# The last stage's plain transfers go from SyncE's queue to GpSimd's, and the order planner gets new transfer costs

## The chip, the cores and the metric

The kernel runs on one core of a Trainium2 chip. The core has five engines that run side by side: TensorE (PE, with its weight loads shown as PEld), VectorE (DVE), ScalarE (ACT), GpSimd (POOL) and SyncE (SP). SyncE does nothing but issue transfers. Transfers between HBM and the on-chip memory (SBUF) are carried out by 16 DMA engines, which serve several queues; in the profile q1 is the queue that SyncE feeds, q10 ScalarE's, q0 GpSimd's, and q8 brings instructions. The metric is the device time of one execution in microseconds (us).

## The reference: what is computed

The forward pass and all gradients of a layer with two branches, for 2048 tokens (S) of 512 channels (D) in bf16:

```python
xn = _layernorm(x)                            # x = A_q
k_shift = sum over 4 lags of k shifted * shift_k
kv  = k_shift * v
y   = causal convolution of kv with ssm_k along the sequence (by FFT of length 4096) + kv * ssm_D
s   = xn * y
h   = sigmoid(xn @ w_gate) * (xn @ w_up)      # F = 1376
g   = silu(h @ w_down)
out = x + s * g
_grads = vjp(grad_out)   # of A_q, A_k, A_v, A_shift_k, A_ssm_k, A_ssm_D, w_gate, w_up, w_down
```

Outputs: out_0 is the result, out_1 to out_3 the gradients of q, k and v (2048 x 512 each), out_4 to out_6 those of the short filter, of ssm_k (512 x 2048) and of ssm_D, out_7 and out_8 those of w_gate and w_up (512 x 1376), out_9 that of w_down (1376 x 512).

## The kernel before, in words

Channels are worked in four groups of 128 (GW, index cg), tokens in eight pairs of 128-token tiles (index q). The FFT is done as matmuls with constant matrices; a group's spectrum is made in two halves, so there are eight spectral tiles n = 2 cg + u. There are three stages.

Stage A (forward) interleaves three streams (L1028): strG (layer norm, gate and up products, one q at a time), strK (spectra of ssm_k) and strV (shifted k, kv, its spectra, and the convolution). It stores to scratch in HBM what is needed again: h to hS_d, the sigmoids to sF_d, both spectra to KK_d (eight tiles of 1 MB), the shifted k to ksh_d.

Stage B (stepB, L1179) goes over the eight q: z_gen makes the gate and the gradient behind it, d_gen the gradients of the gate and up products (stored to dgS_d and duS_d), x_gen the gradient to x (out_1).

The last stage has three streams again. `dW` (L1217) makes the weight gradients out_9, out_7 and out_8 in nine jobs (s, c): s picks hS_d, dgS_d or duS_d, c one of three column chunks of 512, 512 and 352 (CH, L1205). Each job first needs a transposing load of its chunk from HBM (ld_L, L1208, 2 MB for a 512-wide chunk), which goes into one of two buffers, three once job 2 is through; a job frees its buffer and so lets the load three jobs (at first two jobs) later start. A job has four blocks (job 2 has three) of 16 accumulating matmuls; each block is copied out of PSUM into one of three small buffers (ot_r, L1387) and stored (L1243, L1245). `frontC` (L1274) makes the spectra Y of the gradient of the convolution's output. `backC` (L1288) takes for each n the tile KK(n) that ld_KK (L1253) loads into one of two buffers, multiplies both of its halves by Y on VectorE (L1302 to L1306, called M(n) here), and turns the products back with TensorE (inv3, inv1n, inv1). For each pair of groups `taps` (L1324) then makes the gradients of v (out_3), k (out_2) and the short filter; it needs v, k and the shifted k, loaded by ld_bwd (L1263) and ld_ksh (L1259). In the last stage SyncE issues all of these loads and stores; only the eight small copies inside SBUF at L1331 and L1332 are GpSimd's.

The order in which each engine's queue holds its instructions is not the program's. All operations are recorded (class Rec, L163), with a rank that run_streams (L559) gives by mixing the streams: a stream's tuple holds the work that it has, and the times at which it should begin and end as shares of the stage (the numbers at L1400 and L1415 to L1416). Then `order` (L348) plays all engines forward with the estimated costs of `cost` (L291) for compute and `dcost` (L328) for transfers, and takes on every engine the operation of the lowest rank that is ready. That order is emitted (L545) as a fixed program; each engine then does its instructions strictly in that order, and waits at each for what it needs. Line L553 issues all of TensorE's bursts and L555 everything else, so nearly every row of the profile has one of these two lines. A transfer costs the planner the time by which it holds its issuing queue and the time that it holds the DMA engines; `dcost` gives both from the size, the length of the contiguous runs, and the issuing engine:

```python
if "transpose" in meth:
    return (1.4 if str(src.space) != "DRAM" else nb / 215e3), nb / 256 * 18 / 16e3
...
pk = nb / run
d = pk * max(8 + 0.0375 * run, 18) / min(16, pk) / 1e3
```

Of the kernel before, what the change touches and what calls it, by code (L numbers as in the profile page):

```python
# [15 lines left out]
DRAM = bass.MemoryType.DRAM  # L16
# [11 lines left out]
GW = D // NG  # L28
# [134 lines left out]
class Rec:  # L163
# [164 lines left out]
    def dcost(self, alt):  # L328

        eng, meth, a, k = alt  # L330
        dst, src = a[0], a[1]
        nb = math.prod(dst.shape) * esize(dst.dtype)
        if "transpose" in meth:
            return (1.4 if str(src.space) != "DRAM" else nb / 215e3), nb / 256 * 18 / 16e3
        run = 4096 if eng == "sync" else 1 << 13
        for v in (dst, src):
            dims = [d for d in v.ap if d[1] > 1]
            r = 1
            for s, n in reversed(dims if str(v.space) == "DRAM" else [d for d in v.ap[1:] if d[1] > 1]):
                if s != r:  # L340
                    break
                r *= n
            run = min(run, r * esize(v.dtype))
        pk = nb / run
        d = pk * max(8 + 0.0375 * run, 18) / min(16, pk) / 1e3
        return (0.58 + max(0, pk - 256) * 3e-4 if eng == "gpsimd" else 0.55 if eng == "scalar" else 0.36 + max(0, pk - 128) * 6e-4), d

    def order(self):  # L348
# [210 lines left out]
def run_streams(streams, until=None):  # L559

    live = [list(st) + [0.0] * (5 - len(st)) for st in streams]
    while live:
        if until is not None and until():
            break
        for st in sorted(live, key=lambda s: s[2] + (s[3] - s[2]) * s[4] / s[1]):
            try:
                c = next(st[0])
            except StopIteration:
                live.remove(st)
                break  # L570
            if c:
                st[4] += c
                break
        else:
            raise RuntimeError("all streams blocked")
    return live
# [68 lines left out]
def kernel_impl(ctx, tc, A_q, A_k, A_v, A_shift_k, A_ssm_k, A_ssm_D, B_x, B_w_gate, B_w_up, B_w_down,  # L645
                grad_out, out_0, out_1, out_2, out_3, out_4, out_5, out_6, out_7, out_8, out_9):
    nc = tc.nc
    qC, kC, vC, goC = cview(A_q), cview(A_k), cview(A_v), cview(grad_out)
# [3 lines left out]
    ksh_d = dram.tile([NG, P, NJ, GW], bf16, name="ksh_d")  # L652
# [12 lines left out]
    def dma2(eng, dst, src, lo=None):  # L665
        if lo is None:
            for r in range(2):
                eng.dma_start(dst[64 * r:64 * r + 64], src[r])
# [201 lines left out]
    def ld_kh(eng, kh, c0, c1):  # L870
        nc.gpsimd.memset(kh[0:1, 0:3, :], 0.0)
        dma2(eng, kh[:, 3:, :], kC[:, :, :, c0:c1])
        eng.dma_start(kh[64:128, 0:3, :], kC[0, :, 13:16, c0:c1])
        eng.dma_start(kh[1:64, 0:3, :], kC[1, 0:63, 13:16, c0:c1])
# [342 lines left out]
    def dW():  # L1217
        for n, (s, c) in enumerate(jobs):
            f0, w = CH[c]
            while ("L", n) not in stC:  # L1220
                yield 0
            blk = stC.pop(("L", n))
            L = blk.ap
            nblk = -(-w // 128) if s == 0 else 4
            for b in range(nblk):
                acc = nc.ps("hi", [512], f32)
                kf = min(128, w - b * 128) if s == 0 else 128
                wo = D if s == 0 else w
                for j0 in range(0, NJ, 2):
                    calls = []  # L1230
                    for j in (j0, j0 + 1):
                        kw = dict(start=(j == 0), stop=(j == NJ - 1))
                        if s == 0:
                            calls.append(("matmul", (acc[0:kf, :], L[:, j, b * 128:b * 128 + kf], dzA[:, j, :]), kw))
                        else:
                            calls.append(("matmul", (acc[:, 0:w], xnA[:, j, b * 128:(b + 1) * 128], L[:, j, 0:w]), kw))
                    nc.burst("full", 2 * (wo / 2400 + 0.0025), calls)
                    if j0 % 4 == 2 and j0 < 14:
                        yield 4 * wo
                ot = ot_r.next()  # L1240
                nc.evac(ot[0:kf, 0:wo], acc[0:kf, 0:wo], wo)
                if s == 0:
                    nc.sync.dma_start(out_9[f0 + b * 128:f0 + b * 128 + kf, :], ot[0:kf, :])  # L1243
                else:
                    nc.sync.dma_start((out_7 if s == 1 else out_8)[b * 128:(b + 1) * 128, f0:f0 + w], ot[:, 0:w])  # L1245
                if b == nblk - 1:
                    Lfree.append(blk)
                    if n == 2:
                        Lfree.append(dz_r)
                    ld_L()  # L1250
                yield 4 * wo

    def ld_KK(n):  # L1253
        if n < 8:
            KK = KK_r.next()
            nc.sync.dma_start(KK, KK_d[n].rearrange("p t (c x) -> p t c x", c=2))
            stC["KK", n] = KK

    def ld_ksh(cg):  # L1259
        stC["ksh"] = ksh_r.next()  # L1260
        nc.sync.dma_start(stC["ksh"], ksh_d[cg])

    def ld_bwd(cg):  # L1263
        c0 = cg * GW
        if cg % 2 == 0:
            stC["kh"], stC["vg"] = kh_r.next(), vg_r.next()
            dma2(nc.sync, stC["vg"], vC[:, :, :, c0:c0 + 2 * GW])
            ld_kh(nc.sync, stC["kh"], c0, c0 + 2 * GW)
        if cg % 2 == 0:
            ld_ksh(cg)  # L1270
        h = slice((cg % 2) * GW, (cg % 2 + 1) * GW)
        stC["bwd", cg] = (stC["kh"][:, :, h], stC["vg"][:, :, h])

    def frontC():  # L1274
        for n in range(8):
            cg, u = n // 2, n % 2
            c0 = cg * GW + 64 * u
            if u == 0:
                yield from step1n(lambda j: y2A[:, j, c0:c0 + GW])
            U = flip(stA["V"][:, 32 * u:32 * u + 32])  # L1280
            while stC["nY"] + len(YS_r.aps) <= n:
                yield 0
            Y = YS_r.next()
            step3(U, Y)
            stC["Y", n] = Y
            yield 2048

    def backC():  # L1288
        for cg in range(NG):
            c0, c1 = cg * GW, (cg + 1) * GW  # L1290
            B2 = B2_r.next()
            for u in range(2):
                n = 2 * cg + u
                while ("Y", n) not in stC:
                    yield 0
                Y, KK = stC.pop(("Y", n)), stC.pop(("KK", n))
                if u == 0:
                    ld_bwd(cg)
                for t, B in ((0, B1[:, cg % 2]), (1, B2)):
                    C = KK[:, t]  # L1300
                    M = M_r.next()
                    nc.vector.tensor_tensor(M, Y, C[:, 0:1].to_broadcast([P, 2, 1024]), ALU.mult)  # L1302
                    for c in range(2):
                        nc.vector.tensor_tensor(C[:, c], Y[:, c], C[:, 1], ALU.mult)
                    nc.vector.tensor_tensor(M[:, 0], M[:, 0], C[:, 1], ALU.add)
                    nc.vector.tensor_tensor(M[:, 1], M[:, 1], C[:, 0], ALU.subtract)  # L1306
                    inv3([(M[:, 0], 0), (M[:, 1], 1)], u, B)
                    yield 2048
                stC["nY"] = n + 1
                ld_KK(n + 2)  # L1310
            dKT = dKT_r.next()
            inv1n(B2, dKT.rearrange("p (q j) -> p q j", j=32))
            for e in range(2):
                for u in range(2):
                    nc.sync.dma_start(out_5[c0 + 64 * u:c0 + 64 * u + 64].rearrange("(w e) n -> e w n", e=2)[e],
                                      dKT[64 * e + 32 * u:64 * e + 32 * u + 32, :])
            nc.vector.tensor_copy(dDo[:, cg:cg + 1], dKT[:, 0:1])
            yield 4096
            if cg % 2 == 1:
                yield from inv1(B1, y2A[:, :, c0 - GW:c1])  # L1320
                for g in (cg - 1, cg):
                    yield from taps(g)
# [57 lines left out]
    def gated(g, flag):  # L1380
        yield from g
        flags.add(flag)
# [14 lines left out]
        ld_KK(n)  # L1397
    YS_r = Ring(ar, [2, 1024], n=2)
    V_r, U_r = Ring(ar, [64, 32, 2]), Ring(ar, [32, 32, 2], n=2)
    live = run_streams(live + [(dW(), 35 * 8192, 0.96, 1.59), (frontC(), 8 * 4096, 0.94, 1.63)], until=lambda: "B" in flags)  # L1400
    for r in [wgT_r, wuT_r, go_r, dg_r, du_r, dxa_r, dxn_r, u1_r]:
        r.free()
    kh_r = Ring(ar, [NJ + 3, 2 * GW])
# [8 lines left out]
    row4 = Ring(ar, [512]).ap  # L1412
    row6 = Ring(ar, [GW]).ap
    dw, fr = live
    live = run_streams([(dw[0], dw[1] - dw[4], 0.0, 1.0), (fr[0], fr[1], -0.18, 0.6, fr[4]),  # L1415
                        (gated(endC(), "back"), 4 * 20480, -0.08, 0.69)], until=lambda: "back" in flags)  # L1416
    run_streams(live)
    rec.emit()

# [59 lines left out]
```

## Time and profile before

| | |
|---|---|
| median of 3 runs | 534.5 us (531.28 to 534.68) |
| the profiled execution, its own time | 534.16 us |
| its span (first to last instruction) | 532.4 us |
| TensorE clock granted, mean | 0.96 |
| TensorE busy | 468.2 us, 88% |
| VectorE busy | 387.6 us, 73% |
| ScalarE busy | 282.2 us, 53% |
| GpSimd busy | 49.2 us, 9% |
| moved by the DMA engines | 111.21 MB, mean 209 GB/s |
| of it on SyncE's queue q1 | 86.49 MB in 166444 packets |
| of it on GpSimd's queue q0 | 22.75 MB in 6080 packets |

Stage A lies between 0 and about 180 us, stage B between about 180 and 330 us; the last stage begins inside the end of B at about 318 us and runs to the end. "Busy" is the time in which an engine has an instruction in work; TensorE's is partly modelled. A row of the timeline gives the start, the length, the engine (SPq is SyncE's queue issuing), the tensors written and read, how many instructions were merged, and in brackets the idle time ahead of it with what ended it. A row of windows gives for each stretch the busy time of every engine, the granted TensorE clock (1.00 is full), the share of time in which the 16 DMA engines had packets in work (over 1 where packets overlap) and the rate.

### The profile page before, as it was taken

The numbers are of one execution on the slowest core, as the hardware profiler recorded it, in microseconds if no ns is written. First come the engines' busy times: TensorE is split into PE (matmuls) and PEld (weight loads), VectorE is DVE, ScalarE is ACT, GpSimd is POOL, SyncE is SP. The second block draws the span as 40 slices with busy tenths as digits, with TensorE's granted clock in tenths as the row PEclk, the third lists the DMA queues.
The fourth block names the chain that finished last, engine by engine and source line by source line (L and its number), as shares of the span: only waits on it lengthen the run. The fifth ranks groups of instructions, "written<-read, shape, count | busy, mean of one in ns | idle before, by whom it ended". The sixth has DMA issues, their size and how long they took to land. (4 is left out here: it accounts for less than half of the span.)

```text
span 532.4 us, 14325 instructions
## 1 busy us (share of the span) xinstructions
PE 468.2 (88%) x6249; PEld 293.6 (55%) x6289; DVE 387.6 (73%) x622; ACT 282.2 (53%) x353; POOL 49.2 (9%) x84
## 2 busy tenths in 40 slices
PE   3899878999898889999999999978789884849996
PEld 3676656778575555646646646434345434436453
DVE  8677988767777977887977975693985996163552
ACT  5568784766865735435535536385655543133111
POOL 6032332121121000000000000000000100000000
PEclk9899998999999999999999999988989996969999
DMA  8999795664859978795595169999797999996345
GB/s 216 245 309 215 220 256 185 178 212 171 241 167 274 212 203 228 214 276 140 178 263 160 43 171 280 253 257 267 247 232 196 225 243 215 234 231 165 100 110 124
DMA packets 174699, 111.21 MB, mean 209 GB/s; under 512 B 101806, under 2 KB 160908, under 8 KB 173612
## 3 DMA queue, kind: packets, MB, share of 16 engines
q1 hardware_dynamic: 166444, 86.49, 68.8%
q0 software_dynamic: 6080, 22.75, 12.9%
q10 hardware_dynamic: 2112, 1.05, 0.8%
q8 instruction: 49, 0.80, 0.6%
q14 instruction: 14, 0.11, 0.1%
HBM read 38.44 MB, written 46.83 MB: 160 GB/s over the span
## 5 line engine op out<-in xcount | busy, mean ns | idle before, releaser
L553 PE MATMUL psum<-slab 32*128 32x64 bf16 (+9 forms) x6240 | 466.6, 265 | 59.3 <-DVE slab L555 29.0
L553 PEld LDWEIGHTS <-slab 128*128 128x128 bf16 (+5 forms) x6280 | 292.8, 105 | 232.1 <-issue 65.3
L555 ACT CAST slab<-psum 128x1024 bf16<-128x1024 f32 (+3 forms) x257 | 219.5, 905 | 172.9 <-PE psum L553 152.8
L555 DVE TENSOR_TENSOR slab<-slab 128x1024 bf16<-128x1024 bf16 (+5 forms) x327 | 242.5, 792 | 51.6 <-ACT slab L555 15.4
L555 ACT ACTIVATE slab<-psum 128x1024 bf16<-128x1024 f32 (+2 forms) x60 | 50.0, 834 | 68.1 <-PE psum L553 65.2
L555 DVE CAST slab<-psum 128x1024 bf16<-128x1024 f32 (+1 forms) x27 | 32.3, 1204 | 40.3 <-ACT slab L555 24.4
L555 DVE TENSOR_TENSOR slab<-psum,slab 128x1024 bf16<-128x1024 f32 (+2 forms) x28 | 28.2, 1006 | 16.7 <-PE psum L553 15.7
L555 DVE STREAM_TRANSPOSE slab<-slab 128x512 f32<-128x512 f32 x48 | 31.6, 690 | 4.5 <-ACT slab L555 4.5
L555 DVE SCALAR_TENSOR_TENSOR slab<-slab 128x512 bf16<-128x512 bf16 (+1 forms) x48 | 25.0, 531 | 13.4 <-ACT slab L555 13.1
L555 DVE TENSOR_SCALAR slab<-slab 128x1 f32<-128x1 f32 (+9 forms) x63 | 20.5, 366 | 3.6 <-PE psum L553 1.8
L555 POOL DMA_DIRECT2D slab<-slab x8 | 4.3, 543 | 199.6 <-DVE slab L555 199.6
L555 ACT ACTIVATE slab<-slab 128x512 bf16<-128x512 bf16 (+2 forms) x18 | 15.7, 874 | 2.2 <-issue 1.1
L555 POOL MEMSET slab<- 128x128 bf16 (+3 forms) x8 | 3.3, 432 | 140.4 <-DMA out_dram<-slab 137.3
L555 POOL DMA_DIRECT2D KK_d<-slab x16 | 9.0, 560 | 65.5 <-ACT slab L555 63.6
L555 POOL TENSOR_TENSOR slab<-slab 128x1 f32<-128x1 f32 (+1 forms) x20 | 12.8, 646 | 22.4 <-DVE slab L555 16.0
L555 DVE BATCH_NORM_STATS2 slab<-slab 128x6 f32<-128x512 bf16 x16 | 10.4, 677 | 3.5 <-DMA slab<-in_A_q_dram 3.5
L555 POOL DMA_DIRECT2D hS_d<-slab x8 | 8.8, 1105 | 16.1 <-DVE slab L555 9.8
L555 DVE COPY slab<-slab 128x1216 bf16<-128x1216 bf16 (+2 forms) x16 | 7.1, 462 | 0.5 <-DMA slab<-in_A_k_dram 0.2
L555 POOL DMA_DIRECT2D sF_d<-slab x6 | 3.3, 557 | 10.3 <-ACT slab L555 10.1
L555 ACT ACT_TABLE_LOAD x2 | 2.6, 1283 | 2.9 <-issue 2.9
L555 ACT ACTIVATION_READ_ACCUMULATOR slab<-psum 128x1 f32 x16 | 3.1, 196 | 0.0
L555 POOL DMA_DIRECT2D ksh_d<-slab x4 | 2.3, 570 | 8.7 <-ACT slab L555 8.7
(16 smaller groups left out, 16.1 us busy)
## 6 DMA issues: line engine op xcount, KB each, us to landing
out_dram<-slab SPq DMA_DIRECT2D x74, 128.0 KB, 3.7
KK_d<-slab POOLq DMA_DIRECT2D x16, 512.0 KB, 4.3
slab<-KK_d SPq DMA_DIRECT2D x8, 1024.0 KB, 5.5
hS_d<-slab POOLq DMA_DIRECT2D x8, 704.0 KB, 5.6
dgS_d<-slab SPq DMA_DIRECT2D x8, 704.0 KB, 4.0
duS_d<-slab SPq DMA_DIRECT2D x8, 704.0 KB
sF_d<-slab POOLq DMA_DIRECT2D x6, 704.0 KB, 4.5
slab<-sF_d SPq DMA_DIRECT2D x6, 704.0 KB, 8.3
```

The costliest lines, as they stand in the source:

```text
L553: getattr(self.nc.tensor, m)(*[place(v) for v in aa], **{x: place(v) for x, v in kk.items()})
L555: getattr(getattr(self.nc, eng), meth)(*[place(v) for v in a], **{x: place(v) for x, v in k.items()})
```

## The change

Two things change together. In the last stage the stores of out_9, out_7, out_8 and out_5 and the loads of KK_d, ksh_d, v and k are issued by GpSimd (75 transfers); SyncE keeps the transposing loads, the stores of out_2 and out_3, the two small stores of out_4 and out_6, and what stage B issues. And the planner's transfer costs in `dcost` are other ones, as are the streams' beginning and ending times in the last stage, so that the planner gives another order.

```diff
         if "transpose" in meth:
-            return (1.4 if str(src.space) != "DRAM" else nb / 215e3), nb / 256 * 18 / 16e3
+            return (1.4 if str(src.space) != "DRAM" else nb / 178e3), nb / 256 * 23 / 16e3
...
-        d = pk * max(8 + 0.0375 * run, 18) / min(16, pk) / 1e3
+        wide = 0.047 if eng == "sync" else 0.05
+        if eng == "sync" and run == 512 and not (str(dst.space) == "DRAM" and dst.ap[0][0] >= 2048):
+            wide = 0.08
+        d = pk * max(wide * run, 9) / min(16, pk) / 1e3
...
-                    nc.sync.dma_start(out_9[...], ot[0:kf, :])
+                    nc.gpsimd.dma_start(out_9[...], ot[0:kf, :])
-                    nc.sync.dma_start((out_7 if s == 1 else out_8)[...], ot[:, 0:w])
+                    nc.gpsimd.dma_start((out_7 if s == 1 else out_8)[...], ot[:, 0:w])
...
-            nc.sync.dma_start(KK, KK_d[n].rearrange("p t (c x) -> p t c x", c=2))
+            nc.gpsimd.dma_start(KK, KK_d[n].rearrange("p t (c x) -> p t c x", c=2))
...
-        nc.sync.dma_start(stC["ksh"], ksh_d[cg])
+        nc.gpsimd.dma_start(stC["ksh"], ksh_d[cg])
...
-            dma2(nc.sync, stC["vg"], vC[:, :, :, c0:c0 + 2 * GW])
-            ld_kh(nc.sync, stC["kh"], c0, c0 + 2 * GW)
+            dma2(nc.gpsimd, stC["vg"], vC[:, :, :, c0:c0 + 2 * GW])
+            ld_kh(nc.gpsimd, stC["kh"], c0, c0 + 2 * GW)
...
-                    nc.sync.dma_start(out_5[...], dKT[...])
+                    nc.gpsimd.dma_start(out_5[...], dKT[...])
...
-    ... [(dW(), 35 * 8192, 0.96, 1.59), (frontC(), 8 * 4096, 0.94, 1.63)] ...
+    ... [(dW(), 35 * 8192, 0.93, 1.83), (frontC(), 8 * 4096, 0.86, 1.69)] ...
...
-    ... (fr[0], fr[1], -0.18, 0.6, fr[4]), (gated(endC(), "back"), 4 * 20480, -0.08, 0.69) ...
+    ... (fr[0], fr[1], -0.1, 0.54, fr[4]), (gated(endC(), "back"), 4 * 20480, -0.06, 0.7) ...
```

In the built program each queue's transfers are recounted: SyncE has 147 where it had 222, GpSimd 122 where it had 47. TensorE's order differs in stage A (78 of the bursts 34 to 125 of 925 stand at another place), in 22 bursts early in stage B, and in the last stage from burst 550 on; elsewhere it is the same. Copies out of PSUM that may run on either engine are shared out almost as before (three go from ScalarE to VectorE). In the last stage the back transforms of the last tile, n = 7, stand inside job 6 of dW, where before they stood inside job 5: in blocks 0 and 1 of job 6, before in blocks 1 to 3 of job 5. The load of KK(7) stands on GpSimd's queue behind the store of block 2 of job 4.

More of the change, by code (lines that the diff above doesn't have):

```diff
@@ L1242, in dW @@
                 if s == 0:
-                    nc.sync.dma_start(out_9[f0 + b * 128:f0 + b * 128 + kf, :], ot[0:kf, :])
+                    nc.gpsimd.dma_start(out_9[f0 + b * 128:f0 + b * 128 + kf, :], ot[0:kf, :])
                 else:
-                    nc.sync.dma_start((out_7 if s == 1 else out_8)[b * 128:(b + 1) * 128, f0:f0 + w], ot[:, 0:w])
+                    nc.gpsimd.dma_start((out_7 if s == 1 else out_8)[b * 128:(b + 1) * 128, f0:f0 + w], ot[:, 0:w])
                 if b == nblk - 1:
@@ L1314, in backC @@
                 for u in range(2):
-                    nc.sync.dma_start(out_5[c0 + 64 * u:c0 + 64 * u + 64].rearrange("(w e) n -> e w n", e=2)[e],
+                    nc.gpsimd.dma_start(out_5[c0 + 64 * u:c0 + 64 * u + 64].rearrange("(w e) n -> e w n", e=2)[e],
                                       dKT[64 * e + 32 * u:64 * e + 32 * u + 32, :])
@@ L1399, in kernel_impl @@
     V_r, U_r = Ring(ar, [64, 32, 2]), Ring(ar, [32, 32, 2], n=2)
-    live = run_streams(live + [(dW(), 35 * 8192, 0.96, 1.59), (frontC(), 8 * 4096, 0.94, 1.63)], until=lambda: "B" in flags)
+    live = run_streams(live + [(dW(), 35 * 8192, 0.93, 1.83), (frontC(), 8 * 4096, 0.86, 1.69)], until=lambda: "B" in flags)
     for r in [wgT_r, wuT_r, go_r, dg_r, du_r, dxa_r, dxn_r, u1_r]:
@@ L1414, in kernel_impl @@
     dw, fr = live
-    live = run_streams([(dw[0], dw[1] - dw[4], 0.0, 1.0), (fr[0], fr[1], -0.18, 0.6, fr[4]),
-                        (gated(endC(), "back"), 4 * 20480, -0.08, 0.69)], until=lambda: "back" in flags)
+    live = run_streams([(dw[0], dw[1] - dw[4], 0.0, 1.0), (fr[0], fr[1], -0.1, 0.54, fr[4]),
+                        (gated(endC(), "back"), 4 * 20480, -0.06, 0.7)], until=lambda: "back" in flags)
     run_streams(live)
```

## The prediction

> **What bounds the kernel now.** I read the page's busy times first, then windows of 20 us, then the timelines of the engines where TensorE idles, then SyncE's queue there.
>
> ```profile
> span 532.4 us, 14325 instructions
> PE 468.2 (88%) x6249; PEld 293.6 (55%) x6289; DVE 387.6 (73%) x622; ACT 282.2 (53%) x353; POOL 49.2 (9%) x84
> PE   3899878999898889999999999978789884849996
> ```
>
> TensorE is the busiest engine, and stage B and the end are nearly full of it; what a change of the last stage can give back is TensorE's idle time there. The windows say where that is, and show the DMA engines beside it:
>
> ```profile
> 4.00:24.00 20.00, 13.67 (x230) 11.00 (x231) 14.35 (x42) 13.28 (x14) 5.19 (x9) 0.91 1.11 272
> 320.00:480.00 160.00, 129.22 (x2392) 71.46 (x2412) 110.98 (x156) 81.93 (x100) 2.92 (x5) 0.90 1.08 241
> 480.00:532.00 52.00, 47.21 (x541) 25.63 (x543) 24.17 (x29) 11.17 (x21) 2.13 (x4) 0.99 0.50 124
> ```
>
> From 320 to 480 us TensorE works 129.2 of 160 us, so 30.8 us are idle, and the DMA engines are never out of work (share 1.08, 241 GB/s). After 480 TensorE is full and the DMA engines are half idle. The last large hole, with VectorE's row above TensorE's:
>
> ```profile
> 441.58 6.41 DVE L555 TENSOR_TENSOR slab<-slab 128x1024 bf16<-128x1024 bf16 x9
> 465.99 7.18 DVE L555 TENSOR_TENSOR slab<-slab 128x2048 bf16<-128x2048 bf16 x10 [9.89 <-DMA slab<-KK_d]
> ```
> ```profile
> 444.26 2.51 PE L553 MATMUL psum<-slab 32*128 32x64 bf16 x113 [3.45 <-DVE slab L555]
> 448.93 3.10 PE L553 MATMUL psum<-slab 64*64 64x64 bf16 x128 [2.16 <-issue]
> 453.48 11.49 PE L553 MATMUL psum<-slab 32*128 32x64 bf16 x74 [1.46 <-issue]
> 471.42 2.58 PE L553 MATMUL psum<-slab 32*128 32x64 bf16 x72 [6.45 <-DVE slab L555]
> ```
>
> VectorE waits 9.89 us for the tile KK(7), and TensorE, out of the dW work that its order puts ahead, then waits 6.45 us for VectorE's first products. Why the tile is late stands in SyncE's queue:
>
> ```profile
> 436.59 13.07 SPq L555 DMA_TRANSPOSE slab<-duS_d  x1
> 449.76 6.33 SPq L555 DMA_DIRECT2D out_dram<-slab  x5
> 456.18 1.04 SPq L555 DMA_DIRECT2D slab<-KK_d  x1
> 466.03 9.87 SPq L555 DMA_TRANSPOSE slab<-duS_d  x1
> ```
>
> Its buffer was free when M(5) ended: by 441.2 us at the latest, since the products up to 448.0 are M(6)'s. The load went out at 456.18, 15 us later, behind a transposing load of 13.07 us and five stores of 6.33 us, the last waiting for a copy out of PSUM.
>
> **The change part by part.** The sum is made against the profiled execution, 534.16 us (its span and 1.76 us around it). The median of the runs is 0.3 us above that.
>
> KK(7), and the loads like it. On GpSimd's queue the load no longer stands behind transposing loads, but behind the store of dW job 4, block 2. The earliest landing is 441.2 plus the 5.4 us that the other KK loads of this stage took (447), the latest as now plus nothing (466). TensorE needs VectorE's first products, 5.4 us after the landing, when dW runs out at 464.97; so any landing before 459.5 removes the whole wait. From 447 to 459.5 are two thirds of the range, and the new order also puts all of job 5 and three bursts of job 6 ahead of the first use: I take the whole 6.45 us as gone. Ends: 0 and -6.45. What is late next: the transposing load of job 6, now 436.59 to about 452, whose use comes right there.
>
> The clock after that hole. The first 72 small matmuls behind it took 2.58 us; the same kind at full clock took 1.26 us for 80 (row at 382.90). The windows show a granted clock of 0.74 there. Without the hole: -1.3 us; ends 0 and -2.
>
> VectorE's pile. TensorE waits 1.76, 1.53 and 3.45 us (438 to 447 us, 6.74 in all) for VectorE, which from 412 to 448 has no pause of 0.2 us: taps of the first two groups, M(5) and M(6) come at once. The new order puts dW's job 5, blocks 0 and 1, between the uses of M(5), M(6) and M(7), but the work stays (111.0 us of 160). I take a third, -2.2; ends 0 and -6.7.
>
> Transposing loads, alone on SyncE but for out_2, out_3. No row shows TensorE waiting for one. Their cover is dW itself: a job of four blocks takes four times 3.49 us (distance of ScalarE's copies at 457.38 and 460.87), 14.0 us without the FFT work between, and with three buffers a load has two jobs, 28 us. Now one takes about 13 us from issue to landing. Against a full GpSimd queue the row for the worst is k's load in stage A, 2 MB as here, beside the weights on GpSimd's and ScalarE's queues: 23.2 us. That fits into 28 us, and not into one job, which is what job 2 has (two buffers). I take 0, since the FFT work lies between too; ends 0 and +9 (23.2 less 14.0), which is a rival.
>
> Issuing on GpSimd. 75 transfers move. GpSimd has this row for a 512 KB store and this for one of 1408 short runs:
>
> ```profile
> L555 POOL DMA_DIRECT2D KK_d<-slab x16 | 9.0, 560 | 65.5 <-ACT slab L555 63.6 <-issue 1.7
> L555 POOL DMA_DIRECT2D hS_d<-slab x8 | 8.8, 1105 | 16.1 <-DVE slab L555 9.8 <-issue 6.2
> ```
>
> 67 by 0.56 and eight large loads of v and k by up to 1.1 us make 46 us on an engine that has 5.1 us of work after 320 us: hidden, 0. What it is moved past: the eight small copies of L1331 and L1332 now stand behind stores and loads in that queue, and taps waits for them; they land in 2.4 to 3.1 us now, and a 1 MB load ahead would add about 5 to each of four groups. VectorE's idle 23 us after 480 cover two of them; the others fall where dW fills TensorE: 0, ends 0 and +5. The last store goes out on GpSimd: 0.56 for 0.44 us, +0.2 with rounding.
>
> [...]
>
> Nor does VectorE pay: its 128x2048 products take 1215 ns in stage A beside GpSimd's issues and 1219 ns in the last stage without them.
>
> Instruction fetch. In 320 to 480 us TensorE waits 8.2 us on "issue", five pauses of 0.44 to 2.16 us making 5.8 of it; with three busy queues instead of two these could grow by half (+2.9), or shrink as in stage A between 14 and 110 us, where both queues work and TensorE waited 0.4 us (-5.4). I take 0.
>
> Stage A's order. The bursts that move stand between about 30 and 90 us; TensorE's waits from 14 to 110 us sum to 9.9 us, its bound both ways; copies and bursts are the same ones. I take 0, ends -3 and +3 (a third, as a change of order rarely touches all waits).
>
> Sum: 534.16 - 6.45 - 1.3 - 2.2 + 0.2 = 524.4; with 0.3 for the median 524.7, so 525.0 us.
>
> **The rivals.** First, no gain, 534 us: the DMA engines are the limit (share 1.08 over all 160 us), the bytes are the same, and two queues only deal the same service out otherwise; KK(7) comes early, something else as much later. For it: no window from 320 to 480 us has a share under 0.92. Against it: with transposing loads on SyncE beside GpSimd's loads (the window from 4 to 24 us) the rate was 272 GB/s at a like share, 13% over the 241 here, and transfers that nobody waits for yet (stores) can be what comes later. [...]
>
> Second, slower, about 543 us: dW's stores wait behind the loads on GpSimd's queue. There are three store buffers, so a block's copy waits for the store three blocks before; from 3 times 3.49 = 10.5 us from copy to landing on, TensorE stops. A store takes 4.4 us now (median; longest 8.2). Behind a 1 MB load that itself takes 9.79 us, as KK(7)'s did, it lands after 14.2, 3.7 us too late. Eight such meetings (KK(2) to KK(7), v with k twice) make 30 us; where TensorE has FFT work between, half of that: 534 + 15 less the 6.45 of KK(7) is 543. Against it: the wait for a store now stands in SyncE's queue in just the same way (ScalarE waited 2.6 us in all for stores).
>
> Third, 536 to 540: the transposing loads starve, above all job 2's: up to +9 less part of the gain. For it the 23.2 us of k's load; against it the FFT work in job 1's time.
>
> Fourth, 516: all three of VectorE's waits and the fetch pauses go (-6.7 + 2.2 - 4 more).
>
> **How the numbers follow.** Forecast (520 to 529) 0.52; no gain (529 to 538) 0.22; slower by the stores 0.14; starved loads 0.07; more gain 0.05. A measurement of this kernel tells about 1%, 5.3 us, from no change. Faster by over 1% (under 529.2): 0.49 of the forecast, 0.05, and 0.02 of the second case, 0.56. Slower (over 539.8): 0.02 of no gain, 0.14, 0.05 of starved loads, 0.21. Within: 0.23. The range 515 to 541 leaves out about half of the stores' case, some of the starved loads' and a little of the largest gain, under 0.15. The likeliest case's own range is 520 to 529.
>
> **What would show it.** Right: the KK loads go out within 2 us of their buffer's release and VectorE has no wait for KK_d over 3 us; TensorE's work from 320 us to the end has about 10 us less idle; a rate over 250 GB/s in the stage. Wrong: waits of ScalarE for out_dram over 10 us (stores); waits of TensorE for hS_d, dgS_d or duS_d (starved); the same idle total at new places (no gain); a stage B that begins over 3 us earlier or later (stage A's order).

## The result, and the profile after

The changed kernel takes 588.35 us (median of four runs, 578.84 to 601.77) and the kernel before 534.39 us: 1.092 times as long, 95% interval 1.078 to 1.107. Times are medians of all runs, but this ratio and those below are of the fast runs alone (here 578.84 and 586.79 us). It stands for 49 us; the profiled execution is longer and shows 55.7. The forecast was 525.0 us, in a range of 515 to 541. It is wrong in its sign, and by 63 us.

The profiled execution took 589.91 us. From its page, TensorE's busy tenths in 40 slices of 14.7 us (the span is 588.1 us):

```profile
PE   3899798998987999999999884019839975666995
```

The first 22 slices look as before. TensorE worked 155.72 us of the first 180 (before 155.46) and 137.21 us of the next 140 (136.34), so neither stage A nor stage B lost anything. The digits "84019839975666" are in the last stage. Its windows, and under them the same stage before:

```profile
320.00:480.00 160.00, 106.35 (x1742) 53.27 (x1741) 88.73 (x124) 62.96 (x76) 27.48 (x47) 0.85 1.00 179
...
320.00:588.10 268.10, 184.78 (x2944) 96.13 (x2942) 137.59 (x186) 89.84 (x114) 46.19 (x81) 0.85 0.95 167
```
```profile
320.00:532.40 212.40, 176.44 (x2931) 97.09 (x2954) 135.14 (x185) 93.10 (x120) 5.05 (x9) 0.92 0.93 212
```

From 320 to 480 us TensorE gets 106 us of work done where it got 129, and the DMA engines move 179 GB/s where they moved 241, though they show as busy all the time (share 1.00). Read that pair of columns together: here the full share at the low rate is packets that took longer (61 ns of an engine's time each on q1 from 337 to 392 us, before 35; worked out below), not a lack of requests. Now what TensorE waited for from 320 us to the end (total, times, longest, us):

```profile
PE psum L556 <- issue: 36.2, 8, 10.7
PE psum L556 <- DMA slab<-hS_d: 27.3, 1, 27.3
PE psum L556 <- DVE slab L558: 12.8, 10, 4.2
```
```profile
PE psum L553 <- issue: 8.5, 21, 2.2
```

Before, the same list has 8.5 us for issue (the second fence), nothing for a transfer, 16.6 for VectorE and 5.5 for ScalarE (now 0.5). The bill from 320 us to the end of the span: before 212.4 us, 176.4 of them work; after 268.1, 184.8 of them work. The difference of 55.7 us is +27.3 (hS_d), +27.7 (issue), -3.8 (VectorE), -5.0 (ScalarE), +8.3 (the same work done more slowly: granted clock 0.85 in this window, before 0.92), and 1.2 of small gaps. The two kinds of wait are as large as the whole loss, and the slower work is about made up by the waits that shrank. The granted clock is low around the holes: 0.57 from 360 to 400 us.

The 27.3 us is one wait, for the transposing load of dW's second job. SyncE's queue (start, length, instruction):

```profile
337.99 53.88 SPq L558 DMA_TRANSPOSE slab<-hS_d  x1
...
414.71 51.99 SPq L558 DMA_TRANSPOSE slab<-dgS_d  x3
```
```profile
332.53 10.79 SPq L555 DMA_TRANSPOSE slab<-hS_d  x1
```

The lower fence is the same load before. Before, the nine loads held the queue for 6.0 to 13.1 us each; now the one for job 1 held it for 53.9, the three of dgS_d (one row) for 17 each in the mean, and the first of duS_d for 39.3. What GpSimd's queue issued around the first of them, and TensorE's rows that end the two kinds of wait:

```profile
337.06 1.69 POOL L558 DMA_DIRECT2D slab<-in_A_v_dram  x2 [13.02 <-PE psum L556]
...
344.86 0.57 POOL L558 DMA_DIRECT2D slab<-KK_d  x1
```
```profile
394.24 6.04 PE L556 MATMUL psum<-slab 128*128 128x512 bf16 x109 [27.31 <-DMA slab<-hS_d]
...
434.90 5.69 PE L556 MATMUL psum<-slab 64*64 64x64 bf16 x88 [9.27 <-issue]
```

The transposing load was issued within 1 us of the loads of v and ahead of k, KK, ksh and a second KK (5 MB with some stores), and it landed as those had drained. The DMA queues from 337 to 392 us (packets, MB, share of the engines' time), after:

```profile
q1 hardware_dynamic: 10097, 3.51, 70.1%
q0 software_dynamic: 1198, 5.24, 46.8%
```

and the same stretch before, with everything on q1:

```profile
q1 hardware_dynamic: 27121, 13.86, 108.4%
```

8.82 MB moved (160 GB/s) where 13.97 had (254 GB/s). From these rows a packet of q1 (348 bytes in the mean) took 61 ns of an engine's time, before (511 bytes) 35 ns. So the second queue did not only take the transposing load's turn, it also made the whole slower.

### The profile page after: what moved, and what is told of

Read it like the earlier page. It is cut to its first block, busy times and chain, and to the rows that moved or that the text cites. A ratio compares the mean times of both kernels' runs of the same rounds, so it can differ in the third digit from the quotient of the medians.

```text
span 588.1 us, 14369 instructions
## 1 busy us (share of the span) xinstructions
PE 477.7 (81%) x6289; PEld 294.2 (50%) x6289; DVE 390.0 (66%) x625; ACT 279.5 (48%) x350; POOL 91.3 (16%) x159
## 4 chain that ended last, share of the span: by engine, by line
PE 58%; issue 13%; DVE 8%; ACT 8%; DMA 5%; another core or an unknown queue 5%; POOL 2%; SPq 0%; POOLq 0%; DVEq 0%; ACTq 0%
PE psum L556 58%; DVE slab L558 8%; ACT slab L558 8%; DMA out_dram<-slab 4%; DMA slab<-in_A_q_dram 1%; POOL out_dram L558 1%; POOL slab L558 1%; SPq L558 0%; PE psum L558 0%; POOLq L1477 0%; POOLq L558 0%; DVEq L558 0%; ACTq L558 0%
## 5 line engine op out<-in xcount | busy, mean ns | idle before, releaser
L556 PE MATMUL psum<-slab 32*128 32x64 bf16 (+10 forms) x6280 | 476.1, 264 | 104.1 <-issue 37.4
L556 PEld LDWEIGHTS <-slab 128*128 128x128 bf16 (+6 forms) x6280 | 293.4, 103 | 285.8 <-issue 109.5
L558 ACT CAST slab<-psum 128x1024 bf16<-128x1024 f32 (+6 forms) x254 | 217.1, 904 | 230.6 <-PE psum L556 219.4
L558 DVE CAST slab<-psum 128x1024 bf16<-128x1024 f32 (+1 forms) x30 | 35.3, 1186 | 104.2 <-ACT slab L558 85.9
L558 POOL DMA_DIRECT2D out_dram<-slab x51 | 27.1, 534 | 175.0 <-ACT slab L558 142.1
L558 ACT ACTIVATE slab<-slab 128x512 bf16<-128x512 bf16 (+2 forms) x18 | 15.6, 870 | 3.9 <-DVE slab L558 2.8
L558 POOL TENSOR_TENSOR slab<-slab 128x1 f32<-128x1 f32 (+1 forms) x20 | 12.2, 623 | 26.3 <-DVE slab L558 22.7
L558 POOL DMA_DIRECT2D slab<-KK_d x8 | 4.4, 553 | 28.3 <-DVE slab L558 22.4
L558 POOL DMA_DIRECT2D slab<-in_A_k_dram x8 | 6.2, 774 | 0.3 <-issue 0.3
L558 POOL DMA_DIRECT2D slab<-in_A_v_dram x4 | 3.4, 842 | 13.0 <-PE psum L556 13.0
## 6 DMA issues: line engine op xcount, KB each, us to landing
slab<-KK_d POOLq DMA_DIRECT2D x8, 1024.0 KB, 15.6
```

Of the source, the lines that this page charges most:

```text
L556: getattr(self.nc.tensor, m)(*[place(v) for v in aa], **{x: place(v) for x, v in kk.items()})
L558: getattr(getattr(self.nc, eng), meth)(*[place(v) for v in a], **{x: place(v) for x, v in k.items()})
```

## The experiments

The theory (called "sharing by packets" in the later expectations): a transposing load moves in small packets, plain transfers in large ones (in the probe below 4.19 MB are 16448 packets of transposing loads, 576 of long loads, 1152 of short ones: 255 bytes, 7.3 KB and 3.6 KB in the mean). If, with two queues at work, the engines take a packet of each in turn, the transposing load gets a small part of the bytes until the other queue is empty, while in one queue it waits for its turn once and then has the engines to itself. The rivals: the planner's new costs and the new order are at fault; GpSimd's queue is slow in itself; short runs are slow on that queue, whatever runs beside. Ratios are against the kernel before on the same chip, with 95% intervals. In every run but the two gated ones the planner makes its order anew for that run's queues, so the orders of the last stage differ as well (TensorE's weight loads in order_only leave those of the changed kernel at about the 3490th of 6289).

### micro: the pairs of queues alone

A probe that computes nothing of the reference: ten stretches, each a set of loads or stores of 2 or 4 MB a side, closed by a copy on VectorE that waits for all; 6200 small matmuls run beside.

```python
tr(i):    nc.sync.dma_start_transpose(T[i], A_ssm_k)       # 2 MB, here called T
long_(e): e.dma_start(L[i], ...)                           # 8 KB of each partition in one run
short(e): e.dma_start(L[i], cview(A_v)[:, :, c0:c0+256])   # runs of 512 B, as the loads of v and k
```

> Computes nothing of the reference: ten stretches of transfers, each ended by VectorE copies that wait for all of its transfers, while TensorE runs 6200 small matmuls that wait for none of them. Each stretch but the second, fourth, sixth and ninth begins with two transposing loads of 2 MB on SyncE's queue. In order: 1 transposing loads alone; 2 four 1 MB loads with 8 KB runs on GpSimd's queue alone; 3 both together; 4 both on SyncE's queue in turn; 5 the transposing loads with the four loads on ScalarE's queue; 6 four 1 MB loads with 512 B runs on GpSimd's queue alone; 7 those with the transposing loads; 8 sixteen 128 KB stores (1 KB runs) on GpSimd's queue with them; 9 two transposing loads of k as in stage A beside eight 0.5 MB weight loads on GpSimd's queue; 10 four 512 KB stores with 4 KB runs on GpSimd's queue with the transposing loads. Theory 1 (transposing loads starve beside another queue's long packets): stretch 1 takes about 22 us, stretch 2 about 13, stretch 4 about their sum (35), but stretch 3 60 to 110; TensorE's pauses for instructions grow from under 3 to about 10 us in stretch 3. Theory 2 (the queues share the engines fairly and the new order is at fault): stretch 3 takes no longer than stretch 4, 35 us. Whether short runs, stores, and ScalarE's queue do the same is open; stretch 9 should not, by the 272 GB/s of stage A.

Measured, the closing copies of stretches 1 (two T alone), 3 (T with long loads on GpSimd) and 7 (T with short loads on GpSimd); the bracket is the stretch's length:

```profile
45.98 0.45 DVE L82 COPY fen<-big 128x256 bf16<-128x256 bf16 x1 [22.40 <-DMA big<-in_A_ssm_k_dram]
...
96.37 0.45 DVE L82 COPY fen<-big 128x256 bf16<-128x256 bf16 x1 [33.27 <-DMA big<-in_A_ssm_k_dram]
...
246.43 0.45 DVE L82 COPY fen<-big 128x256 bf16<-128x256 bf16 x1 [55.48 <-DMA big<-in_A_ssm_k_dram]
```

Long loads alone took 14.2 us, so with T the sum would be 36.6, and it took 33.3: nothing is lost, as in one queue or with ScalarE's (32.6 each). Theory 1's 60 to 110 us for that stretch was missed, and theory 2's 35 met. Short loads (23.6 us alone) with T took 55.5 us where the sum is 46.0. Stretch 9, the pair of stage A, took 42.3 us, with 7.4 us of TensorE's pauses for issue. TensorE never stopped for issue in stretches 1 to 5, and for 15.6 us in stretch 7. Inside it, the packets from 212 to 220 us:

```profile
q0 software_dynamic: 360, 1.31, 86.2%
q1 hardware_dynamic: 363, 0.09, 10.9%
```

One packet for one packet: T gets 0.09 MB of 1.4. The second hardware queue (ScalarE's, stretch 5, 140 to 144 us) does the same to it:

```profile
q10 hardware_dynamic: 169, 1.25, 98.1%
q1 hardware_dynamic: 168, 0.04, 9.4%
```

In both windows the two queues moved the same number of packets within 1%, as the theory has it. The count is not even everywhere: in the same stretch 7, from 194 to 206 us,

```profile
q1 hardware_dynamic: 2132, 0.55, 72.4%
q0 software_dynamic: 182, 0.68, 53.8%
```

and both queues are slow, 104 GB/s together where T alone had 189 and the short loads alone 182. In the real kernel (360 to 376 us) 1088 packets of q1 stand against 475 of q0, but in bytes 0.28 MB against 2.24. So the sharing says who gets the bytes. Why the two together can move less than either alone it does not say, and that stays open.

### order_only, queue_only: the two halves of the change

```diff
 order_only:  all of after's costs and stream times; the last stage's transfers back on nc.sync
 queue_only:  before's costs and stream times; the transfers on nc.gpsimd as in after
```

> The new planner costs and stream times, with all of the last stage's transfers back on SyncE's queue. Theory 1 (two queues beside transposing loads): about as before, 525 to 545 us. Theory 2 (the new order): most of the loss stays, 570 us or more.

> The old planner costs and stream times, with the last stage's plain transfers on GpSimd's queue. Theory 1: slow, 570 us or more, with TensorE's waits on the fetch of instructions and for a transposing load near those of the changed kernel (36 and 27 us). Theory 2: 525 to 545 us.

order_only took 532.27 us, ratio 0.995 (0.990 to 1.000); its transposing loads took 6.3 to 12.3 us. queue_only took 577.93 us, ratio 1.064 (1.056 to 1.071); its TensorE waited 48.0 us for issue, and its transposing loads took 14.9 to 29.0 us each (rows of two or three of them 45). TensorE's wait for a transposing load was 4.3 us there, not near the 27 expected: nearly the whole loss of this run is pauses for issue. The new costs and stream times are not at fault; the queue is, under either set of them.

### loads_only, stores_only, vk_only, vk_back, kk_only: which transfers

```diff
 loads_only:  KK, ksh, v, k on gpsimd; stores on sync
 stores_only: stores on gpsimd; all loads on sync
 vk_only:     v, k on gpsimd; the rest on sync
 vk_back:     after, with v, k back on sync
 kk_only:     KK, ksh on gpsimd; the rest on sync
```

> The changed kernel with the stores of out_5, out_7, out_8 and out_9 back on SyncE's queue; the loads of KK_d, ksh_d, v and k stay on GpSimd's. Theory 1 with the loads at fault: 570 us or more. If the stores in GpSimd's queue are at fault: 530 to 545 us.

> The changed kernel with all loads back on SyncE's queue; the stores of out_5, out_7, out_8 and out_9 stay on GpSimd's. Both theories: no loss, 522 to 540 us; if stores in GpSimd's queue matter too, 550 us or more.

> The changed kernel with everything but the loads of v and k back on SyncE's queue. Theory (short runs in GpSimd's queue): most of the loss with 8 of the 75 large transfers moved, 560 us or more. Rival (any load): 535 to 548 us, by their share of the bytes.

> The changed kernel with only the loads of v and k (512 B runs) back on SyncE's queue; KK_d, ksh_d and the stores stay on GpSimd's. Theory (short runs in GpSimd's queue): the loss is gone, 520 to 545 us, TensorE's waits for instructions under 15 us and no transposing load over 20 us. Rival (any load in GpSimd's queue starves the transposing loads): 560 us or more.

> As after, but only the KK and ksh loads (8 KB and 4 KB of each partition in one run) stay on GpSimd's queue; v and k loads and all stores are back on SyncE's. If the classes add up as vk_back less stores_only has it, +3.6%: 553 to 561 us. If long runs cost nothing beside transposing loads, as the probe's stretches 3 and 9 have it (their time is the sum of the parts): 530 to 542 us. By the sharing of packets the transposing loads beside a KK load are held up by its 3 to 5 us each, 8 times, and late loads have some slack: 535 to 553 us.

| on GpSimd's queue | us | ratio | TensorE waits: issue, hS_d (us) |
|---|---|---|---|
| stores_only | 543.73 | 1.010 (1.006 to 1.015) | 9.3, 0 |
| vk_only | 547.84 | 1.017 (1.011 to 1.022) | 7.0, 7.7 |
| kk_only | 550.05 (540.41 to 554.16) | no interval | 12.5, 3.3 |
| vk_back | 564.24 | 1.046 (1.042 to 1.051) | 31.9, 1.2 |
| loads_only | 574.38 | 1.056 (1.048 to 1.063) | 25.1, 14.1 |

The theory that the short loads of v and k carry the loss fell twice: without them the loss is still 4.6%, and by themselves they cost 1.7%. kk_only's median lies in the third of its bands, but its runs, beside runs of before from 532.95 to 546.94, touch all three and decide little. What the table does say: stores alone cost 1.0%, v and k 1.7%, KK with the stores 4.6, KK with v and k 5.6, all three 9.2, more than a plain sum would give (4.6 and 1.7, or 5.6 and 1.0). A backlog that the classes make longer together would explain that; it is argued and not shown, since each run has its own order. And in vk_back, as in queue_only, TensorE hardly waits for a transposing load (1.2 us): the loss comes with the pauses for issue, 31.9 us.

### micro2: which runs, which queue

The probe again (nothing of the reference), with other pairs: short loads alone on SyncE's and on ScalarE's queue; T with short loads on ScalarE's queue and in SyncE's own; T with runs of 1, 2, 4 and 8 KB on GpSimd; T with short and long loads mixed on GpSimd.

> Computes nothing of the reference: ten stretches like those of the first probe, beside 7000 small matmuls. Short loads are four times 1 MB with 512 B runs (v and k as the last stage loads them). In order: 1 short loads on SyncE's queue alone; 2 on ScalarE's queue alone; 3 two transposing loads (4 MB) on SyncE's with short loads on ScalarE's; 4 both on SyncE's queue in turn; 5, 6, 7 the transposing loads with 4 MB of loads on GpSimd's queue in runs of 1, 2 and 4 KB; 8 with 4 MB on GpSimd's, short and 8 KB runs in turn; 9 with 8 KB runs alone (33.0 us in the first probe); 10 with one short and one 8 KB load. Theory (short runs in GpSimd's queue are the cause: 180 GB/s alone and 55.5 us beside the transposing loads in the first probe): stretch 1 about 14 to 20 us, stretch 4 about 40 us, 5 near 55, 7 near 35, 8 over 45, and TensorE's pauses for instructions only where short runs are on GpSimd's queue (5, 8, 10). Rival (short runs are as slow on any queue): stretch 1 takes 23 us like GpSimd's, stretches 3 and 4 55 us.

Short loads alone took 22.7 us on either hardware queue, as on GpSimd's (23.6): they are slow (185 GB/s), but not because of that queue. With T they took 42.3 us in SyncE's own queue, 44.4 on ScalarE's, and 55.5 on GpSimd's in the first probe. On GpSimd with T, runs of 1 KB took 44.6, 2 KB 35.4, 4 KB 33.2 and 8 KB 34.3 us. The theory's bands for short loads alone (14 to 20) and for 1 KB (near 55) were missed, and so was the rival's 55 for stretches 3 and 4; pauses for issue of up to 1.7 us came in stretch 3 too, with nothing on GpSimd's queue. 2 MB of short with 2 MB of long loads on GpSimd beside T took 57.8 us, where the parts make some 41 (22.4 for T, half of 22.7, half of 14.2); with 1 MB of each they took 47.6, where the parts make some 32. In the first of these two, from 292 to 320 us, T's packets are down to 9 to 24 GB/s while q0 has work; once it had none, from 328 to 332 us, T ran at 286 GB/s. TensorE's longest pause for issue, 13.61 us, is in that stretch too.

### act_loads: another second queue

```diff
 loads_only, with
-            nc.gpsimd.dma_start(KK, KK_d[n]...)      # and ksh, v, k
+            nc.scalar.dma_start(KK, KK_d[n]...)
```

> As after, but the last stage's KK, ksh, v and k loads are issued on ScalarE's queue and the stores on SyncE's: loads_only with another second queue. Theory one, sharing by packets, whichever the second queue is: the transposing loads still stand still beside it (stretch 5 of the probe: 168 against 169 packets in 140 to 144 us), some of them take over 25 us, TensorE waits for hS_d or dgS_d, and the time is 555 us or more. Theory two, GpSimd's queue is the cause: transposing loads of 6 to 14 us, and 540 us or less. What blurs it: ScalarE itself waits in front of a load whose buffer is not free; its waits for anything but TensorE are then to be taken off.

578.08 us, ratio 1.072 (1.060 to 1.084). The transposing load of job 1 took 33.43 us (before 10.79), here beside v and KK on ScalarE's queue; SyncE's row, and ScalarE's:

```profile
337.72 33.43 SPq L558 DMA_TRANSPOSE slab<-hS_d  x1
```
```profile
337.65 2.02 ACTq L558 DMA_DIRECT2D slab<-in_A_v_dram  x2
```

dW's stores stood behind that load on SyncE's queue, and ScalarE waited 33.9 us for one of their buffers. So ScalarE's queue, a hardware one, starved the transposing load as well, though TensorE's own wait for hS_d was only 1.7 us. The size is blurred, as expected, by work that ScalarE itself held up: with those 33.9 us off it would be near 544, less than the 555 that the theory asked for; the other waits for issue (20.8 us) are near those of loads_only (25.1).

### t_gate, t_gate2: the same queue, without the overlap

Both are loads_only with the same order on the other engines. In t_gate GpSimd copies one element of the last transposing load's block into a load's target before it issues it; in t_gate2 also one element of its last load into the next transposing load's target. The copies are overwritten; each load waits for what it would overtake.

```diff
+ if transposing load of dW:  gpsimd.tensor_copy(its target[0], last load[0])     # t_gate2 alone
+ if large load on gpsimd:    gpsimd.tensor_copy(its target[0], last transposing load[0])
```

> As loads_only (KK, ksh, v and k loads on GpSimd's queue, stores on SyncE's, the same order on every other engine), but GpSimd copies one element of the last transposing load's block into the first element of each load's target before it issues that load (19 copies), so that a load cannot start while an issued transposing load is under way. Theory one, sharing by packets: a transposing load of 256-byte packets gets one packet for each packet of 4 to 8 KB of another queue, as the probe's stretch 7 shows (363 against 360 packets in 212 to 220 us), so it stands still while another queue has work; with the overlap taken away the transposing loads take 16 us or less in the median, TensorE's wait for hS_d falls under 5 us, and the time is 555 us or less (loads_only 574). Theory two, GpSimd's queue is slow in itself, with or without overlap: 565 us or more, TensorE's pauses for issue still 25 us.

573.3 us, ratio 1.060 (1.045 to 1.076): inside the rival's band, with 26.8 us of pauses for issue. TensorE's wait for hS_d went, and six of the nine transposing loads took 6.1 to 9.6 us, but three took 14.0, 28.0 and 37.7 us: five loads went out at 350.7 to 357.6 us beside the one issued at 350.4. The gate was open on its other side, and by its time the run tells nothing apart.

> t_gate with the other half of the gate: before each transposing load GpSimd also copies one element of its last large load into the first element of that transposing load's target, so the transposing load waits for the loads ahead of it as well as they for it (27 copies of one element in all). No large load of GpSimd's queue overlaps a transposing load any more; queue, order and bytes are those of loads_only. In t_gate one pair still overlapped: five loads issued at 350.7 to 357.6 us beside the transposing load issued at 350.4, which took 28 us. Sharing by packets as the cause: no transposing load over 16 us (from its own start), no wait of TensorE for hS_d over 3 us, pauses for issue down to 15 us or less from 25, and 535 to 558 us, what remains being waits of the loads for each other. GpSimd's queue slow in itself: pauses for issue still 25 us or more, and 565 us or more.

557.39 us, ratio 1.039 (1.032 to 1.046), where loads_only has 1.056 (1.048 to 1.063) with the same queue, order and bytes: about 9 us less. All nine transposing loads took 5.4 to 9.8 us. TensorE's two waits in loads_only, and the waits in t_gate2, from 318 us on:

```profile
PE psum L556 <- issue: 25.1, 6, 9.3
...
PE psum L556 <- DMA slab<-hS_d: 14.1, 1, 14.1
```
```profile
DVE slab L569 <- DMA slab<-KK_d: 39.1, 4, 15.7
...
PE psum L557 <- DVE slab L569: 33.7, 10, 8.6
...
PE psum L557 <- issue: 5.8, 18, 1.6
```

No wait for hS_d, and the pauses for issue, 25.1 us in loads_only, are 5.8, none over 1.6. Both kinds of wait that make up the loss hang on the overlap, then, and not on GpSimd's queue in itself; this is shown for the loads, as the stores were not gated. What is left, 3.9%, is by the rows the gate's own price: KK comes late (39.1 us of VectorE's waits), and TensorE waits 33.7 us for VectorE (before 16.6) and 12.4 for ScalarE (before 5.5), at a granted clock of 0.86 (before 0.92).

## Why the prediction was wrong

The step that failed first is "Transposing loads", taken as 0 with ends 0 and +9; it measured 27.3 us of waiting, for a load of 54 us. The row chosen for the worst, 23.2 us for k's load in stage A, was the right kind of row and was read wrongly: as how slow such a load can be. It was only how long the weights' loads kept their queues busy. The trace of the kernel before shows that: from 14 to 18 us, with GpSimd's weight loads at work,

```profile
q0 software_dynamic: 261, 0.90, 71.7%
q1 hardware_dynamic: 284, 0.07, 9.3%
```

and from 20 us, when q0 was empty, k's load ran at 290 GB/s. Beside 5 MB of other loads the load of job 1 took 53.88 us, and TensorE, out of other work at 366.9 us, had covered 29 of them. The third rival had this cause, at 7% and at +9 us, and its sign, TensorE's wait for hS_d, is the one that came.

The second is "Instruction fetch", taken as 0 with ends -5.4 and +2.9; it measured +27.7 us. TensorE stopped at 425.6 us and went on at 434.90; in between, the one instruction packet of 16 KB took 1.07 us but started only at 432.4 us, 6.8 us into the pause. All seven pauses over 2 us are of this kind: each holds one such packet, and TensorE goes on 1.2 to 1.7 us after the packet's end. Stage A's 0.4 us of such waits, from 14 us on, was no bound: it has the large transposing load beside GpSimd's weight loads only until about 19 us (from 19 to 20 us only q1 has packets, 1133). That the overlap causes the pauses is shown (25.1 us of them in loads_only, 5.8 in t_gate2; in the first probe none with transposing loads alone, 3.3 us with short loads alone on GpSimd's queue, 15.6 with both); why that packet started 6.8 us late is not, and stays open.

The third, "The clock after that hole", taken as -1.3, has its sign turned: with the new holes the granted clock falls from 0.92 to 0.85, and the same work takes 8.3 us longer.

Right in kind: KK(7)'s wait is gone (VectorE waits for no KK_d; of GpSimd's 28.3 us of idle time ahead of these loads 22.4 ended with VectorE and 5.8 with TensorE). There is luck in it: the loads now take 15.6 us (median) where the other KK loads took 5.4, in a stage that has become 56 us longer, and KK(7), issued at 485.92, was first used at 514.32. The size was not right: all of TensorE's waits for VectorE fell from 16.6 to 12.8 us, by 3.8, where KK(7) and VectorE's pile together were taken as 8.65. Stage A's order gave nothing. Issuing on GpSimd is as cheap as taken: a KK load 553 ns, a half of v 842.

Of the rivals, the second had the right sign and the wrong mechanism: ScalarE waited 2.6 us for out_dram and VectorE 9.5, not 30, and TensorE for neither. The first held that two queues only deal the same service out otherwise; no bandwidth was won, but some was lost, and 254 GB/s became 160 (337 to 392 us). Against that rival stood the window from 4 to 24 us with 272 GB/s. It shows that a mixture can be fast, as the probe's long loads are (257 GB/s in stretch 3); it says nothing of who gets the bytes.

The best version measured is order_only, all of the last stage's transfers on SyncE's queue with the new costs: 0.995 of the kernel before, with an interval that ends at 1.000.

## What to carry to other kernels

A queue is also an order of service: in these runs a transfer waited once behind others in the same queue (KK(7) 15 us in the kernel before), while beside a second queue it shared by packets, and one with small packets (a transposing load) got little until the other queue was nearly empty (0.28 MB against 2.24 from 360 to 376 us in the changed kernel). That alone need not cost time (T with long loads in the probe: 33.3 us where the sum is 36.6), but it does when that transfer is the one waited for (27.3 us for hS_d). So before moving transfers to a second queue, ask which one is needed first and which has the larger packets, and take as the bound of the small one the time that the other queue will have work. A row in which a load was slow beside another queue gave the length of that queue's backlog, not a worst case: 23.2 us beside the weights in stage A, 53.88 beside 5 MB in the last stage.

## What the runs showed of the hardware

- Two queues with work got equal counts of packets in some stretches of the probe: 363 against 360, and 168 against 169, whether the second queue is GpSimd's or ScalarE's. In others the count was uneven and both were slow (2132 against 182, 104 GB/s together). A transposing load with no other packets beside it ran at 286 GB/s (micro2, 328 to 332 us), two of them with their gaps at 189 (stretch 1 of the first probe); beside another queue with work at 9 to 24 in the mixed stretch of micro2, 11 in stretch 7 of the first probe (0.09 MB in 8 us) and 18 in the changed kernel (0.28 MB in 16 us).
- Loads in runs of 512 B reached 182 to 185 GB/s alone on any of three queues. Beside a transposing load they took about the sum on the hardware queues (44.4 and 42.3 us for 45) and 9.5 us more than the sum on GpSimd's (55.5 for 46.0). Why GpSimd's differs here was not found.
- Instruction fetch came late while two queues had work: in the two longest pauses of the changed kernel (9.27 and 10.67 us) the instruction packet started 6.8 and 8.2 us in. TensorE's pauses for issue were up to 13.6 us in a probe (short and long loads mixed beside a transposing load); there were none with runs of 2, 4 or 8 KB alone on GpSimd's queue beside a transposing load. In the kernel short loads are not needed for it: without v and k on that queue (vk_back) the pauses were still 31.9 us in all.
